# An mLSTM and mixture layer on one core: weight bytes, weights converted ahead, third tile and old-state products

## The chip, the cores and the metric

The kernel runs on one core of a Trainium2 chip. The metric is device time in microseconds of one execution, taken as a median of several runs. TensorE multiplies (PE in the rows; PEld is its weight load), VectorE (DVE), ScalarE (ACT) and GpSimd (POOL) do the rest of the arithmetic. SyncE (SP) and ScalarE issue DMAs, each from a queue of its own.

## What is computed

The reference runs an mLSTM recurrence over 768 tokens for each of 4 batches x 8 heads with a head size of 40, gates the result, and puts it through a two-layer feed-forward block.

```python
for t in range(S):
    m_new = np.maximum(f_gate[:, :, t] + m, i_gate[:, :, t])
    f_stab = np.exp(f_gate[:, :, t] + m - m_new)
    i_stab = np.exp(i_gate[:, :, t] - m_new)
    m = m_new
    C = f_stab * C + i_stab * einsum('bhd,bhe->bhde', vt, kt)
    n = f_stab * n + i_stab * kt
    h_tilde = einsum('bhde,bhe->bhd', C, qt)
    denom = np.maximum(np.abs(einsum('bhd,bhd->bh', n, qt)), 1.0)
    y[:, :, t] = sigmoid(o_gate[:, :, t]) * h_tilde / denom
h = x @ w_in                                   # (3072, 320) @ (320, 2048)
g = np.maximum(h, 0.0) + np.log1p(np.exp(-np.abs(h)))
out = (g @ w_out).astype(np.float32)           # @ (2048, 320)
```

The weights arrive as 64-bit floats and are made into f32 on the chip.

## The kernel before

*Tiles and steps.* The recurrence is cut into chunks of 128 tokens. One step is one chunk of one batch with its 8 heads, named batch_chunk: 0_1 is batch 0, chunk 1. There are 24 steps; three make a token tile of 384 tokens, and there are 8 tiles (NT), numbered from 0. `ORDER` (L38) sets which step is which: tile 0 is 1_0, 2_0, 0_0; tile 1 is 3_0, 0_1, 0_2; tile 2 is 0_3, 0_4, 0_5; the later tiles follow batches 1, 2 and 3. A step with chunk above 0 needs the state of the chunk before it.

*A step.* Decay factors are broadcast from DRAM (`fb`, L435) and scanned into a decay matrix `pw` (L444, two halves). The scores q.k (`sp`) are weighed by it (L536). The weighed scores times the gated values give `yq` (L607). Where there is an old state, its product with q (`iq`) is multiplied by the decays `y` that were loaded from DRAM (`fc_d`, L357), and `yq` is added (L613). The result `y` goes to DRAM (`yd`, L620) and comes back in the layout of the activations (`nw`, `yx`, L627 to L635). The denominator `nm` (L639 to L641) scales the gate `eg` (L644), which multiplies `yx` (L650). ScalarE casts that into X (L652), VectorE writes the remainder into X's second half (L654). The new state is `cn` (L517).

*Three forms of step.* Tile 0 (`first_tile`) has no old state and works in plain f32. Tile 1 (`mid`, `scores_pairs` and `inter_pairs`, L556 and L587) also takes q and k in f32, with two heads stacked on partitions 0 and 64. From tile 2 on (`wide`, t >= WIDE), q and k are loaded (L297), split into a high part on ScalarE (L302) and a remainder on VectorE (L308), and stacked three times by six DMAs on the chip per step (L392, L393), so that one pass of TensorE does the three products; the state is stacked and split in the same way (L326, L327, L523, L524).

*The feed-forward block.* For each tile and each of 16 slices of the hidden size, 8 matmuls make `hp` (L941), ScalarE applies softplus (L812, L816, L817), VectorE forms the remainder `gl` (L820), and `po` gathers the second layer (L912): 3 matmuls in f32 for tile 0, 9 in split form later. In tile 0's slices the weights are still on their way. There are 16 weight tensors, 8 of each layer (`wi`, `wo`), loaded by L229 into three raw buffers. Each is made into f32 words by `single` (L199): two scaled copies (L206, L212) and one operation on the top byte of each word (L210) on ScalarE, then a merge on VectorE (L215). For wi, casts and remainders follow (L239 to L249), for wo a cast (L259) and later a remainder (L268).

*What sets the order.* Every engine runs its instructions in the order in which they were written. Tile 0's beginning is ordered by the table `F`. From its first product on, `tick` counts matmuls, and attention steps, conversions, output copies and loads are generators that resume when their due count comes. The due counts are in the tables `W` (wide steps), `M` (tile 1), `Q`, `CI` and `CO` (wi and wo conversions). `tensors` (L876) is the order of the weight tensors, and the first `AHEAD` of them are converted from within `F`. The y of tile 1 has one buffer (`yy`, L352); that of a wide step shares the three raw weight buffers (L354). Tile t's products are written after all three of its steps have ended (L926).

## Time and profile before

| | |
|---|---|
| median of 3 runs | 495.15 us (490.76 to 496.38) |
| the profiled execution's own time | 490.26 us |
| its span, first to last instruction | 488.5 us |
| TensorE busy | 457.8 us (94%), 3309 matmul records |
| VectorE busy | 326.7 us (67%) |
| ScalarE busy | 226.1 us (46%) |
| GpSimd busy | 74.4 us (15%) |
| granted TensorE clock, mean | 0.962 |

Times in a row are counted from the span's start. An f32 matmul stands as two records. A wait is put down to the releaser that came last. The granted clock is a share of full speed: 1.00 is 2.4 GHz, 0.50 is 1.2 GHz.

### The profile page before, as it was taken

To read this page: it belongs to the slowest core of one execution; us is meant where nothing else is said; L and a number is where in the kernel's file an instruction comes from. 1 tells how busy PE (TensorE), PEld (TensorE's weight loads), DVE (VectorE), ACT (ScalarE), POOL (GpSimd) and SP (SyncE) were. 2 spreads that over 40 slices of the span, in tenths; PEclk is the share of its full clock that TensorE was granted. 3 is DMA by queue.
4 is the path that set the end of the run, shared out by engine and by line. 5 is a ranking of instruction groups with operands and counts; after the bars stand their busy time and mean duration, and the time that the engine had idled before them with its cause. 6 is when DMAs were issued, how large, how long until landed. Compare 5 with 4: busy or idle time off the path is not lost.

```text
span 488.5 us, 8914 instructions
## 1 busy us (share of the span) xinstructions
PE 457.8 (94%) x3309; PEld 429.0 (88%) x3309; DVE 326.7 (67%) x581; ACT 226.1 (46%) x427; POOL 74.4 (15%) x133
## 2 busy tenths in 40 slices
PE   7888988777999979999999999999998999999997
PEld 7776755566998979999999999999997999999996
DVE  5868676858699646878679667867785765642211
ACT  3469676863443523535343634264243533334232
POOL 4131301120210220310130220212031021000000
PEclk9759988988999979999999999999999999999999
DMA  6927887672686864765696666766674563001001
GB/s 223 366 82 266 265 274 232 227 216 74 189 232 177 218 176 113 215 166 169 200 250 162 202 175 186 221 192 193 167 225 125 180 185 109 16 23 42 1 1 40
DMA packets 75482, 82.79 MB, mean 169 GB/s; under 512 B 5975, under 2 KB 62191, under 8 KB 75439
## 3 DMA queue, kind: packets, MB, share of 16 engines
q1 hardware_dynamic: 55237, 72.58, 49.2%
q10 hardware_dynamic: 20202, 9.64, 8.1%
q8 instruction: 26, 0.43, 0.4%
q14 instruction: 17, 0.14, 0.1%
HBM read 54.49 MB, written 8.40 MB: 129 GB/s over the span
## 4 chain that ended last, share of the span: by engine, by line
PE 65%; DMA 17%; DVE 7%; ACT 5%; SPq 3%; issue 2%; ACTq 1%; POOL 0%; DVEq 0%
PE hp L941 28%; PE po L912 27%; DMA fb<-fz_d 3%; DMA yx<-yd 3%; PE yq L607 3%; DMA y<-fc_d 2%; PE sp L543 2%; DMA yd<-y 2%; DVE pw L444 2%; DMA kst<-hik 1%; PE yp L573 1%; DMA qst<-hiq 1%; DMA qst<-loq 1%; PE iq L547 1%; DMA nw<-yd 1%
## 5 line engine op out<-in xcount | busy, mean ns | idle before, releaser
L941 PE MATMUL hp<-X,wih 128*128 128x384 f32 x768 | 185.3, 348 | 7.4 <-ACT X L652 6.0
L941 PEld LDWEIGHTS hp<-X,wih 128*128 128x128 f32 x768 | 136.8, 192 | 11.8 <-ACT X L652 6.5
L816 ACT ACTIVATE gh<-hp 128x384 fp32r<-128x384 f32 x112 | 55.0, 491 | 192.1 <-PE hp L941 171.9
L820 DVE TENSOR_TENSOR gl<-hp,gh 128x384 fp32r<-128x384 f32 x112 | 60.8, 551 | 46.0 <-ACT hp L817 45.3
L912 PE MATMUL po<-woh,gl 128*128 128x320 f32 x336 | 70.5, 312 | 2.0 <-DVE gl L820 1.8
L912 PE MATMUL po<-wol,gh 128*128 128x320 f32 x336 | 72.2, 314 | 0.0
L912 PE MATMUL po<-woh,gh 128*128 128x320 f32 x336 | 72.0, 312 | 0.0
L941 PE MATMUL hp<-X,wil 128*128 128x384 f32 x256 | 67.7, 344 | 0.0
L912 PEld LDWEIGHTS po<-woh,gh 128*128 128x128 f32 x336 | 58.1, 189 | 0.3 <-issue 0.3
L912 PEld LDWEIGHTS po<-woh,gl 128*128 128x128 f32 x336 | 54.8, 189 | 2.8 <-DVE gl L820 2.8
L444 DVE TENSOR_TENSOR_SCAN pw<-fb,ident 128x512 f32<-128x512 f32 x48 | 56.0, 1206 | 1.2 <-PE fb L430 1.1
L912 PEld LDWEIGHTS po<-wol,gh 128*128 128x128 f32 x336 | 54.8, 189 | 0.7 <-issue 0.7
L817 ACT ACTIVATE hp<-hp 128x384 f32<-128x384 f32 x112 | 54.5, 486 | 0.0
L536 DVE TENSOR_TENSOR pw<-sp,pw 128x512 f32<-128x512 f32 x48 | 32.6, 685 | 31.4 <-PE sp L543 31.2
L327 POOL TENSOR_TENSOR cs<-cn,cs 120x336 fp32r<-120x336 f32 x15 | 14.2, 945 | 224.2 <-ACT cs L326 179.3
L941 PEld LDWEIGHTS hp<-X,wil 128*128 128x128 f32 x256 | 47.0, 191 | 0.8 <-issue 0.7
L912 PE MATMUL po<-wof,gh 128*128 128x320 f32 x96 | 33.5, 493 | 7.8 <-DVE wof L215 7.8
L912 PEld LDWEIGHTS po<-wof,gh 128*128 128x128 f32 x96 | 19.2, 211 | 16.9 <-DVE wof L215 9.1
L553 DVE TENSOR_TENSOR y<-iq,y 41x512 f32<-41x512 f32 x36 | 24.4, 679 | 1.6 <-DMA y<-fc_d 1.0
L607 PE MATMUL yq<-pw,vi 128*48 128x128 f32 (+1 forms) x336 | 23.0, 280 | 1.1 <-DVE pw L536 1.0
L457 POOL TENSOR_TENSOR vi<-vt,gT 128x328 f32<-128x328 f32 x23 | 20.3, 884 | 15.2 <-DMA vt<-in_vko 7.7
L652 ACT CAST X<-eg 128x384 fp32r<-128x384 f32 x21 | 10.7, 508 | 22.0 <-DVE eg L650 22.0
(118 smaller groups left out, 508.3 us busy)
## 6 DMA issues: line engine op xcount, KB each, us to landing
fb<-fz_d SPq DMA_DIRECT2D x44, 256.0 KB
vt<-in_vko SPq DMA_DIRECT2D x23, 324.0 KB
qst<-hiq SPq DMA_DIRECT2D x36, 160.0 KB
kst<-hik SPq DMA_DIRECT2D x36, 160.0 KB
wi<-in_wts SPq DMA_DIRECT2D x8, 640.0 KB
wo<-in_wts SPq DMA_DIRECT2D x8, 640.0 KB
eg<-in_oT SPq DMA_DIRECT2D x7, 576.0 KB
yd<-y ACTq DMA_DIRECT2D x42, 96.0 KB
```

The costliest lines, as they stand in the source:

```text
L327: nc.gpsimd.tensor_tensor(z.cs, z.old, z.cs, op=ALU.subtract)
L444: nc.vector.tensor_tensor_scan(pw.rearrange(flat), fb.rearrange(flat), ident4.rearrange(flat), 0.0, ALU.mult, ALU.add)
L457: nc.gpsimd.tensor_tensor(z.vi, v1, gT[:, z.c, z.hs].unsqueeze(2).broadcast_to([128, H, E]), op=ALU.mult)
L536: nc.vector.tensor_tensor(z.pws[i], sp, z.pws[i], op=ALU.mult)
L553: nc.vector.tensor_tensor(y, iq, y, op=ALU.mult)
L607: nc.tensor.matmul(yq[e0:e1, p, :], z.via[:, h * E : h * E + e1 - e0], z.pws[i][:, p, :], start=True, stop=True)
L652: nc.scalar.copy(X[:, 0:3, ts], z.e)
L816: nc.scalar.activation(gh, hp, AF.Softplus)
L817: nc.scalar.activation(hp, hp, AF.Softplus)
L820: nc.vector.tensor_tensor(gl, hp, gh, op=ALU.subtract)
L912: nc.tensor.matmul(po[j], a[:, j * 128 : (j + 1) * 128], w, start=first, stop=(last and left[j] == 0))
L941: nc.tensor.matmul(hp, a, r, start=(i == 0), stop=(i == len(seq) - 1))
```

## The change

Four things change, and with them the numbers of all the tables.

1. The operation on the top byte (L210) moves from ScalarE to GpSimd. It adds a large constant, so that the byte lands in the low bits of the f32 word; ScalarE then overwrites the upper half word (L212), which therefore waits for GpSimd.
2. `AHEAD` goes from 1 to 3, so two tensors of the first layer and one of the second are converted from within `F`. Tile 2's output gates are loaded and put through the sigmoid there too.
3. `PLAIN` and `WIDE` go from 2 to 3: tile 2 is treated as tile 1 is, with a table `N` of its own. Its y keeps the buffers and the DMA queue of the wide steps (`late`); tile 1's y is now written and read back through SP's queue (`queue`). Loads of q and k in this form take 104 partitions instead of 128.
4. `inter_pairs` goes. `scale_queries` multiplies q by the decays in one VectorE operation, and `values_wide` adds the old state's products to the value products in PSUM. For this the states of chunks 0_0 to 0_4 lie in two fixed tiles `chain` with zeros between the heads' blocks.

```diff
-PLAIN = 2
-WIDE = 2
+PLAIN = 3
+WIDE = 3
...
-        half = sg.bitcast(U16).rearrange("p (f w) -> p f w", w=2)
-        nc.scalar.activation(half[:, :, 0], top, AF.Copy, scale=1.0 / 32, bias=-31.0 / 64)
-        yield
-        nc.scalar.activation(half[:, :, 1].bitcast(F16), hi_w.bitcast(F32), AF.Copy, scale=2.0**-112)
+        half = sg.bitcast(F16).rearrange("p (f w) -> p f w", w=2)
+        nc.gpsimd.tensor_scalar(sg.bitcast(F32), top, -15.5, 1.5 * 2.0**28, op0=ALU.add, op1=ALU.add)
+        yield
+        nc.scalar.activation(half[:, :, 1], hi_w.bitcast(F32), AF.Copy, scale=2.0**-112)
...
-    F = dict(wm=16, g0=10, l0=19, w00=86, l1=45, g1=50, fz=71, o0=93, l2=122, lg0=15, f2=116, o1=122, w10=210,
+    F = dict(wm=16, zs=212, g0=10, l0=19, w00=46, l1=51, g1=49, fz=71, o0=93, l2=116, lg0=7, f2=116, o1=122, o2=315,
...
-            self.wide, self.mid = self.t >= WIDE, self.t == 1
+            self.wide, self.mid = self.t >= WIDE, 0 < self.t < WIDE
...
-            self.at = W if self.wide else M
-            self.split = NG <= nxt < 2 * NG
+            self.at = (M, M, N, W)[min(self.t, WIDE)]
+            self.late = self.t > 1
+            self.queue = nc.scalar if self.late else nc.sync
+            self.split = NG <= nxt < WIDE * NG
...
-            nc.sync.dma_start(z.qst, qk2[z.s, 0])
-            nc.sync.dma_start(z.kst, qk2[z.s, 1])
+            nc.sync.dma_start(z.qst[0 : PP + D], qk2[z.s, 0, 0 : PP + D])
+            nc.sync.dma_start(z.kst[0 : PP + D], qk2[z.s, 1, 0 : PP + D])
...
-    def inter_pairs(z):
-        rows = [slice(i * PP, i * PP + E) for i in range(2)]
-        iqs = [ps_a.tile([PP + E, HG, L], F32, tag="pa", name=f"iq{i}_{z.n}") for i in range(2)]
-        z.old = z.old or last_state(z)
-        for p in range(HG):
-            for i, old in enumerate(halves(z.old, True, E)):
-                q = z.qst[i * PP : i * PP + D, p, :]
-                nc.tensor.matmul(iqs[i][rows[i], p, :], old[:, p, :], q, start=True, stop=True)
-        for i in range(2):
-            yield Q["IQD"]
-            nc.vector.tensor_tensor(z.y[rows[i]], iqs[i][rows[i]], z.y[rows[i]], op=ALU.mult)
-            done.add(("iq", z.s, i))
+    def scale_queries(z):
+
+        rows = slice(0, PP + D)
+        nc.vector.tensor_tensor(z.y[rows], z.qst[rows], z.y[rows], op=ALU.mult)
+        done.add(("iq", z.s, 0))
+        done.add(("iq", z.s, 1))
...
+        joint = z.mid and z.c > 0
+        if joint:
+            need(("iq", z.s, 0))
+            z.old = z.old or last_state(z)
+        for p in range(HG):
+            rows = [(yq[i * PP : PP + i * EP, p, :], PP + i * (EP - PP)) for i in range(2)]
+            for i, (y, m) in enumerate(rows):
+                h = 2 * p + i
+                nc.tensor.matmul(y, z.via[:, h * E : h * E + m], z.pws[i][:, p, :], start=True, stop=not joint)
+            for i, (y, m) in enumerate(rows if joint else []):
+                nc.tensor.matmul(y, z.old[:, i, p, 0:m], z.y[0 : PP + D, p, :], start=False, stop=True)
...
-            nc.scalar.dma_start(rows[i], z.y[i * PP : i * PP + EP])
+            z.queue.dma_start(rows[i], z.y[i * PP : i * PP + EP])
...
-            eg[1] = p1.tile([128, NG, 3, L], F32, tag="eg", bufs=2, name="eg1")
-            nc.sync.dma_start(eg[1], oT[1])
+            for t in range(1, WIDE):
+                eg[t] = p1.tile([128, NG, 3, L], F32, tag="eg", bufs=2, name=f"eg{t}")
+                nc.sync.dma_start(eg[t], oT[t])
+                yield
+            for t in range(1, WIDE):
+                nc.scalar.activation(eg[t], eg[t], AF.Sigmoid)
+                done.add(("eg", t))
             yield
...
-    AHEAD = 1
+    AHEAD = 3
```

The change of tables and code moves instructions on every engine. Three places follow; line numbers of the changed kernel are about 6 to 16 higher than those of the same lines before.

The first is ScalarE's queue before the first product. `sgi` and `sgo` are words of a tensor of the first or second layer in the making, `eg` the output gates of a tile, `X` the activations of tile 0. Before:

```order
L693 ACTIVATE eg_172<-eg_172 128x1152
L702 ACT_TABLE_LOAD
L664 CAST X_315<-xp_0_316 128x3x128
L239 CAST wih<-sgi_258 128x2x256
L243 CAST wih<-sgi_258 64x128 x2
L664 CAST X_315<-xp_0_327 128x3x128
L664 CAST X_315<-xp_0_339 128x3x128
L206 ACTIVATE magi_356<-wi_208 128x640
L210 ACTIVATE sgi_358<-wi_208 128x640
```

And now:

```order
L718 ACT_TABLE_LOAD
L705 ACT_TABLE_LOAD
L705 ACTIVATE eg_174<-eg_174 128x1152
L705 ACTIVATE eg_299<-eg_299 128x1152
L206 ACTIVATE magi_304<-wi_210 128x640
L212 ACTIVATE sgi_310<-wi_210 128x640
L239 CAST wih<-sgi_310 128x2x256
L243 CAST wih<-sgi_310 64x128 x2
L206 ACTIVATE mago_351<-wo_176 128x640
L212 ACTIVATE sgo_353<-wo_176 128x640
L672 CAST X_339<-xp_0_340 128x3x128
L259 CAST woh<-wof_350 128x640
```

Two more weight tensors (`wi_210`, `wo_176`), a second tile of gates and a second table load stand ahead of X, and the byte operation (L210) stands nowhere.

The second is VectorE's queue in tile 0, around the merge for slices 10 and 11 (`wof_989` before, `wof_946` now). `pw_3` are the scans of step 0_3, `y_2` step 0_2's result, `X` the activations of tile 1. Before:

```order
L644 TENSOR_TENSOR eg_172<-eg_172,nm_1_945 128x384
L444 SCALAR_TENSOR_TENSOR pw_3_0_969<-fb_3_0_880,ident_79 128x512
L444 SCALAR_TENSOR_TENSOR pw_3_1_971<-fb_3_1_882,ident_79 128x512
L613 TENSOR_TENSOR y_2_825<-yq_2_959,y_2_825 112x512
L517 TENSOR_TENSOR cn_2_937<-cn_2_937,cp_2_950 40x4x41 x2
L650 TENSOR_TENSOR eg_172<-yx_1_850,eg_172 128x384
L654 TENSOR_TENSOR X_818<-eg_172,X_818 128x3x128
L215 SCALAR_TENSOR_TENSOR wof_989<-mago_990,sgo_997 128x640
```

And now:

```order
L652 TENSOR_TENSOR eg_174<-eg_174,nm_1_905 128x384
L623 COPY y_2_824<-yq_2_919 112x512
L247 TENSOR_TENSOR wil<-sgi_844,wih 128x2x256
L249 TENSOR_TENSOR wih<-sgi_844,wih 64x128 x2
L658 TENSOR_TENSOR eg_174<-yx_1_835,eg_174 128x384
L526 TENSOR_TENSOR chain_103<-chain_103,cp_2_910 40x4x41 x2
L662 TENSOR_TENSOR X_778<-eg_174,X_778 128x3x128
L215 SCALAR_TENSOR_TENSOR wof_946<-mago_947,sgo_949 128x640
```

The scans of step 0_3 have gone behind the merge (they stand six rows further down), and the remainders of a first-layer tensor have come ahead of it.

The third is SP's queue at step 0_1 of tile 1. `y_1` are its decays, `yd_0` the written result of step 3_0, `nw_0` and `yx_0` what is read back of it. Before:

```order
L229 DMA wi_580<-in_wts 128x1280
L189 DMA flast<-fl_d 104x160
L528 DMA park<-cn_0_529 40x336
L297 DMA loq_596<-in_qk 120x1024
L297 DMA lok_598<-in_qk 120x1024
L229 DMA wo_607<-in_wts 128x1280
L357 DMA y_1_612<-fc_d 64x4x128
L358 DMA y_1_612<-fc_d 48x4x128
L382 DMA qst_2_636<-in_qk 128x512
L383 DMA kst_2_637<-in_qk 128x512
L229 DMA wi_654<-in_wts 128x1280
```

And now:

```order
L229 DMA wo_622<-in_wts 128x1280
L363 DMA y_1_633<-fc_d 64x4x128
L364 DMA y_1_633<-fc_d 48x4x128
L388 DMA qst_2_637<-in_qk 104x512
L389 DMA kst_2_638<-in_qk 104x512
L189 DMA flast<-fl_d 104x160
L635 DMA nw_0_669<-yd_0_581 128x1x128
L229 DMA wi_678<-in_wts 128x1280
L641 DMA yx_0_671<-yd_0_581 128x2x128
L643 DMA yx_0_671<-yd_0_581 128x1x128
L229 DMA wo_710<-in_wts 128x1280
L628 DMA yd_1_744<-y_1_633 192x1x128 x2
```

The loads of tile 2's q and k (`loq`, `lok`) are gone, and the reads of `yd_0`, with the write of `yd_1` behind them, stand between the weight loads.

## Rows read from the trace of the kernel before

**Rows 1.** Stages: length, busy PE, PEld, DVE, ACT, POOL (x instructions), clock, DMA share, GB/s
```profile
61.90:117.20 55.30, 42.36 (x281) 31.79 (x280) 39.88 (x69) 38.73 (x61) 6.74 (x12) 0.91 0.73 226
...
173.00:182.00 9.00, 5.91 (x21) 5.90 (x21) 4.18 (x9) 1.87 (x4) 1.44 (x2) 0.62 0.74 211
182.00:228.40 46.40, 46.40 (x380) 45.32 (x380) 34.10 (x62) 20.93 (x40) 8.51 (x17) 1.00 0.62 172
...
sum 488.50, PE 457.76 PEld 428.98 DVE 326.72 ACT 226.13 POOL 74.45; mean PE 65.39 PEld 61.28 DVE 46.67 ACT 32.30 POOL 10.64
```

**Rows 2.** Timeline, TensorE: start, us, line, operation [idle before <-releaser]
```profile
64.65 1.06 PE L594 MATMUL iq<-qst,cn 40*41 40x128 f32 x14 [2.33 <-DVE pw L536]
...
100.62 4.92 PE L912 MATMUL po<-wof,gh 128*128 128x320 f32 x12 [4.52 <-DVE wof L215]
...
117.21 1.97 PE L941 MATMUL hp<-X,wih 128*128 128x384 f32 x5 [2.93 <-ACT X L652]
...
176.10 1.97 PE L941 MATMUL hp<-X,wih 128*128 128x384 f32 x5 [3.09 <-ACT X L652]
```

**Rows 3.** TensorE's busy time, granted clock, DMA share, in low stretches
```profile
66.00:69.40 3.40, 3.40 (x30) 0.50 0.96 318
...
175.20:182.00 6.80, 5.89 (x20) 0.50 0.73 217
```

**Rows 4.** Timeline, ScalarE and VectorE ahead of the wait at 100.62 us
```profile
91.15 1.16 ACT L369 ACTIVATE eg<-eg 128x1152 f32<-128x1152 f32 x1
...
92.32 1.28 ACT L371 ACT_TABLE_LOAD   x1
...
98.73 0.51 ACT L652 CAST X<-eg 128x384 fp32r<-128x384 f32 x1 [1.30 <-DVE eg L650]
...
99.75 0.82 DVE L215 SCALAR_TENSOR_TENSOR wof<-mago,sgo 128x640 uint32<-128x640 uint32 x1
```

**Rows 5.** Groups of instructions: busy us, mean ns | idle before, releasers
```profile
L607 PE MATMUL yq<-pw,vi 128*48 128x128 f32 (+1 forms) x336 | 23.0, 280 | 1.1 <-DVE pw L536 1.0
...
L543 PE MATMUL sp<-qst,kst 120*128 120x128 f32 x144 | 20.4, 264 | 0.0
...
L547 PE MATMUL iq<-qst,cs 120*41 120x128 f32 x144 | 14.6, 223 | 1.0 <-DVE y L553 1.0
...
L564 PE MATMUL sp<-qst,kst 40*128 40x128 f32 x96 | 8.8, 335 | 2.4 <-DMA kst<-in_qk 2.4
...
L210 ACT ACTIVATE sgi<-wi 128x640 uint16<-128x640 uint8 x8 | 7.4, 924 | 0.0
...
L206 ACT ACTIVATE magi<-wi 128x640 f32<-128x640 f32 x8 | 6.3, 783 | 2.3 <-DMA wi<-in_wts 2.2
...
L239 ACT CAST wih<-sgi 128x512 fp32r<-128x512 f32 x8 | 5.0, 619 | 3.6 <-DVE sgi L215 3.6
```

**Rows 6.** Timeline, GpSimd products and a VectorE merge beside one
```profile
6.94 1.94 POOL L163 TENSOR_TENSOR ig<-ig,m 32x640 f32<-32x640 f32 x1 [4.51 <-DVE m L160]
...
36.19 0.74 POOL L457 TENSOR_TENSOR vi<-vt,gT 128x328 f32<-128x328 f32 x1 [2.84 <-DMA vt<-in_vko]
...
36.31 1.30 DVE L215 SCALAR_TENSOR_TENSOR wof<-mago,sgo 128x640 uint32<-128x640 uint32 x1 [0.72 <-ACT sgo L212]
```

**Rows 7.** Timeline, VectorE and TensorE before the first product
```profile
19.21 1.28 DVE L536 TENSOR_TENSOR pw<-sp,pw 128x512 f32<-128x512 f32 x2
...
24.36 0.17 DVE L577 TENSOR_SCALAR nq<-yp 128x8 f32<-128x8 f32 x1 [1.47 <-PE yp L573]
...
31.71 0.69 PE L941 MATMUL hp<-X,wih 128*128 128x384 f32 x1 [0.57 <-ACT X L664]
```

**Rows 8.** Chain that ended last: start us, us, what
```profile
52.03 9.17 DMA yd<-y
...
195.58 1.39 PE hp L941 x8
196.97 1.32 PE po L912 x9
```

More of the change, by code (lines that the diff above doesn't have):

```diff
@@ L294, in prepare @@
         parts[t] = []
-        for nm, src in zip("qk", qk[t - 2]):
+        for nm, src in zip("qk", qk[t - WIDE]):
             lo = p1.tile([D3, H, L], F32R, tag=f"lo{nm}", name=f"lo{nm}{t}")
@@ L350, in load_decays @@
         need("fc") if z.c > 0 else None
-        if z.mid:
+        if not z.late:
             z.y = p1.tile([PP + EP, HG, L], F32, tag="yy", name=f"y{z.n}")
@@ L480, in halves @@
         if split:
-            return [tile[i * PP : i * PP + D, :, 0:e] for i in range(2)]
+            return [tile[i * PP : i * PP + D, i, :, 0:e] for i in range(2)]
         return [tile[0:D, i, :, 0:e] for i in range(2)]
     def old_state(z):
-        shape = [PP + D, HG, E2] if z.split else [D3, 2, HG, E2]
-        z.cn = p2.tile(shape, F32, tag="cn" if stays(z.b, z.c) or z.s > NG else "cs", name=f"cn{z.n}")
+        if z.split:
+            z.cn = chain[z.c % 2]
+        else:
+            tag = "cn" if stays(z.b, z.c) or z.s > NG else "cs"
+            z.cn = p2.tile([D3, 2, HG, E2], F32, tag=tag, name=f"cn{z.n}")
         z.new = halves(z.cn, z.split, E)
@@ L603, in values_wide @@
         yq = ps_a.tile([PP + EP, HG, L], F32, tag="pa", name=f"yq{z.n}")
-        for h in range(H):
-            p, i = divmod(h, 2)
-            e0, e1 = i * PP, PP + i * EP
-            nc.tensor.matmul(
-                yq[e0:e1, p, :], z.via[:, h * E : h * E + e1 - e0], z.pws[i][:, p, :], start=True, stop=True
-            )
+        joint = z.mid and z.c > 0
[9 more added lines that the diff above has]
+                nc.tensor.matmul(y, z.old[:, i, p, 0:m], z.y[0 : PP + D, p, :], start=False, stop=True)
         yield Q["YQD"]
-        if z.c > 0:
+        if z.c > 0 and not joint:
             need(("iq", z.s, 0), ("iq", z.s, 1))
@@ L626, in read_wide @@
         z.nq = p1.tile([128, L], F32, tag="sig", name=f"nw{z.n}")
-        nc.scalar.dma_start(z.nq, z.yd[DM : DM + H].partition_broadcast(128 // H))
-        if z.mid:
+        z.queue.dma_start(z.nq, z.yd[DM : DM + H].partition_broadcast(128 // H))
+        if not z.late:
             z.yx = p1.tile([128, 3, L], F32, tag="x", name=f"yx{z.n}")
@@ L669, in new_x @@
         Xs[t] = p2.tile([128, 6, T], F32R, tag="X", name=f"X{t}")
+    chain = [cpool.tile([PP + D, 2, HG, PP], F32, name=f"chain{i}") for i in range(2)]
     def first_tile():
@@ L689, in next_gates, with zeros @@
         def next_gates():
-            eg[1] = p1.tile([128, NG, 3, L], F32, tag="eg", bufs=2, name="eg1")
-            nc.sync.dma_start(eg[1], oT[1])
+            for t in range(1, WIDE):
[5 more added lines that the diff above has]
+                done.add(("eg", t))
             yield
-            nc.scalar.activation(eg[1], eg[1], AF.Sigmoid)
-            done.add(("eg", 1))
-            yield
+        def zeros():
+            for c in chain:
+                nc.gpsimd.memset(c, 0.0)
         def keep_decays():
@@ L797, in later_step @@
                 (Q["F6"] if z.s == WIDE * NG else W["FB"], fetch),
-                (Q["L9"] if z.s == (WIDE + 1) * NG else W["LOAD" if z.g else "LOAD0"], lambda: load(z)),
+                (W["LOAD" if z.g else "LOAD0"], lambda: load(z)),
                 (W["SP1"], lambda: scores(z, 1, 0)),
@@ L991, in mlstm_moe_kernel @@
         for t in range(WIDE, NT):
-            start(wide_gates([t]), TS * (t - 2) + Q["GT" if t > WIDE else "GT2"])
+            start(wide_gates([t]), TS * (t - 2) + Q["GT"])
         zs = first_tile()
```

60 lines of the change are left out of this document (32 added, 28 removed).

## The prediction

> **What bounds the kernel now.** I read the busy time by stage first, then TensorE's waits in each stage, then the other engines around those waits.
>
> TensorE is busy 457.76 of 488.5 us, but not evenly [rows 1]. From 182 to 228.4 us it is busy for all of 46.40 us at a granted clock of 1.00. Nothing off TensorE is worth anything in that stage, and it repeats for most of the span. Before it, TensorE is fed badly. From 61.9 to 117.2 us, the second part of token tile 0's products, it is busy 42.36 of 55.30 us, so idle for 12.94, at a clock of 0.91. From 173 to 182 us, around the start of tile 2, it is busy 5.91 of 9.00 us at 0.62.
>
> Its longest waits [rows 2] are of three kinds: for VectorE's merge of an output weight (wof, L215), 4.52 us at 100.62; for the weighing of an attention step (pw, L536), 2.33 us at 64.65; and for the activations X that start a tile (L652), 2.93 us at 117.21 and 3.09 us at 176.10. Behind the long waits the clock is lower. Five stretches after 61.9 us stand at 0.50: three of 3.4 us before 117 us, one of 3.4 us at 117.2, one of 6.8 us at 175.2; the first and the last of them stand in [rows 3]. Work at half clock takes twice its time, so a stretch costs half its length: 1.7 us four times, and 3.4 us.
>
> The 4.52 us wait shows why the merges are late [rows 4]. In ScalarE's queue stand a sigmoid of tile 2's output gates (1.16 us), a table load behind it (1.28 us) with a twin ahead of it, and byte operations on weights (0.92 us each, L210) [rows 5]. In VectorE's queue, ahead of the merge at 99.75 us, stand two scans for the next step and the end of step (0,1), which itself waits for ScalarE's cast of X at 98.73 us.
>
> **The change part by part.**
>
> *Byte operation to GpSimd (16 instructions of L210).* ScalarE loses 0.92 us a tensor [rows 5], 14.7 us in all, about 12 of it after the first product. GpSimd gains an operation of one strided byte input that the trace does not show. From below: a product of 328 elements with two inputs took 0.74 us [rows 6]; half the reads make 0.37, and 640 elements 0.72. From above: 640 elements with two inputs took 1.94 us [rows 6]. I take 1.0, nearer to the 0.74 row, whose shape (128 partitions) is the nearer one. GpSimd is busy 6.74 of 55.30 us in the stage [rows 1], so its idle time hides 11 to 13 of them; only ScalarE's half-word write, which now waits for GpSimd, could be held up.
>
> There is a second cost. VectorE's merge took 0.82 us at 99.75 [rows 4], but 1.30 us at 36.31, while GpSimd's product ran from 36.19 [rows 6]: 0.48 us lost to the overlap. Thirteen more GpSimd operations behind the first tensors, every second one of them meeting such a VectorE operation, make 13 x 0.5 x 0.5, about 3 us of VectorE time. I count that in what remains below. The Trainium skill ("SBUF — State Buffer", section "SBUF: two separate sides") speaks against the edit: a VectorE operation with two SBUF inputs and a GpSimd operation that reads SBUF lock each other out for a whole instruction. The overlapped merge agrees. By that rule the 13 could cost VectorE up to 13 us, which is the VectorE rival below.
>
> *Three tensors converted ahead.* Three weight tensors instead of one are converted before the first product, and two tiles' gates go through the sigmoid there, behind a softplus table load that has come ahead of them, so that a further load follows (first order piece in the section on the change). VectorE's second merge now stands ahead of the second step's denominators. The path: VectorE's first weighing pairs end at 20.49 [rows 7]; merge 0.82; casts 0.62, and two of a quarter of its elements, together as long again; two table loads 2.56; two sigmoids 2.32; conversion of the second tensor 0.78 and 0.92 [rows 4, 5]; its merge 0.82. The sum is 29.95 us. The denominators started at 24.36, so what stands behind them comes 5.5 us later, and the first product at about 37.2 instead of 31.71 us [rows 7]. From below this costs 2.5 us (had the strict chain an overlap of half of it), from above 7, if the third tensor's merge and cast, which stand among the last casts of X, come on top. I take **+5.5**. In return two tensors more are done by then.
>
> *Tile 2 in f32, old-state products in the value products.* Gone for tile 2: the split of q and k, 18 on-chip stacking DMAs, and the copies and casts of each state. VectorE has one multiplication less in each of five steps with an old state (two by iq become one by q). TensorE's work hardly moves [rows 5]: a wide step has 1.13 us of scores (20.4/18) and 0.81 of old-state products (14.6/18), an f32 step 1.47 (8.8/6) and, in the form of the value products, 1.10 (23.0/21). That is +0.63 for each of three steps. In tile 1 two steps go from 1.2 (1.06 for 14 of 16 records [rows 2]) to 1.10. Together **+1.7 us**.
>
> *SP queue.* Tile 1's y writes and reads move from ScalarE's DMA queue to SP. There the waiting DMA held conversions; here it holds weight loads and the next step's decays (third order piece). One such write took 9.17 us to land [rows 8], and SP already waited for it before it loaded the next decays, because tile 1's y buffer is single. Cost from -2 (ScalarE no longer held) to 9 us; I take 0, with the three raw weight buffers as the cover.
>
> *The sum, against the profiled execution's own 490.26 us (span 488.5).*
> - Start: +5.5.
> - Stage 61.9 to 117.2: 12.94 idle and 3 x 1.7 of low clock make 18.0 to win. The scans stand behind the merge now (second order piece), ScalarE has about 12 us less to do and no sigmoid pair, and one tensor less is left to convert. VectorE stays the fullest engine after TensorE (39.88 of 55.30 [rows 1]), so I leave a third: **-12**.
> - Start of tile 1: the 2.93 is in that stage; half of the low clock's 1.7: -0.9.
> - Start of tile 2: 3.09 and 3.4. The values of its last step now stand in product group 9 of tile 1 instead of 11, so two groups more lie between them and X, 2 x 2.71 us (1.39 + 1.32 [rows 8]), against 3.09 missing: **-6**.
> - TensorE's work: +1.7.
>
> 5.5 - 12 - 0.9 - 6 + 1.7 = -11.7, so **478.6 us**. Later tiles are bound by TensorE before and after and give nothing. The three timed runs before lie from 490.76 to 496.38 with a median of 495.15; the profiled one is 4.9 below that. I do not add the difference and leave it to the range's upper part.
>
> **The rivals.**
>
> *VectorE becomes the bound.* For: it is the next fullest engine in the stage, and each lockout with GpSimd is added there. Against: five multiplications and tile 2's split go. With 10 us lost in place of 3, 7 of the 12 won are given back: 486 us.
>
> *SP's queue takes the place of ScalarE's.* For: a write takes 9.17 us to land, and twice as many such waits now stand between weight loads. Against: loads run up to three tensors ahead. If the merges come as late as before, the 12 and the 0.9 are not won: 490.3 + 5.5 - 6 + 1.7 = 491.5 us.
>
> *GpSimd's byte operation is far dearer than any of its rows (slower).* It takes every eighth byte and converts it. Place: ScalarE's half-word write behind it, 13 times in tile 0. With 13 operations of c us and GpSimd's other 8 or so, tile 0's products end no sooner than 37 + 8 + 13c. They ended near 114, so above c = 5.5 us the stage grows, and above about 6 it takes back tile 2's 6 us too. At c = 7 tile 1 starts at 136 instead of 117, and the time is 490.3 + 19 - 6 + 1.7 = 505 us. Against: that is over three times the upper bound from rows.
>
> **How the numbers follow.** Forecast 0.64 (own range 468 to 485); VectorE 0.15 (486); SP 0.13 (491.5); GpSimd 0.08 (505). About 1% is what a measurement of this kernel can tell from no change, so faster is below 490.2 against the median of 495.15. The forecast, VectorE and 0.02 of SP's spread make 0.81 faster; 0.10 of SP the same; GpSimd with 0.01 of SP 0.09 slower. The range reaches down to 466, where all of 18.0, 1.7 and 6.5 is won, the start costs 2.5 and TensorE's work nothing (466.6), and up to 491, about SP's time.
>
> **What would show it.** Right: the first product near 37 us; no wait for wof over 2 us before tile 1; tile 1 starting between 105 and 113 us; no low clock where tile 2 starts, near 163 us; byte operations near 1 us. Wrong: tile 1 starting at 117 us or later; merges of 1.3 us and more as a rule (VectorE); weight loads that SP issues late behind y, with merges waited for as now (SP); byte operations of several us (GpSimd); a first product after 39 us.

## The result, and the profile after

The changed kernel takes 479.51 us (median of 4 runs, 478.38 to 481.38); the kernel before, run beside it, 495.76 us (490.76 to 500.64). The ratio is 0.971, with a 95% interval of 0.963 to 0.979. A control later, the changed kernel once more on another occasion, gave 479.53 us (476.09 to 480.83) and a ratio of 0.969 (0.963 to 0.975). The profiled execution took 481.38 us (span 479.6). The ratios here and below leave out disturbed executions, those over 1.5% above the fastest of their kernel, so that a ratio need not be that of the two medians.

Windows of the two traces, cut at the first product of tile 0, at the starts of tiles 1, 2 and 3, and at the end; the kernel before comes first. Columns as in [rows 1].

```profile
0.00:31.70 31.70, 25.64 (x152) 23.03 (x152) 23.04 (x49) 12.79 (x20) 10.76 (x21) 0.79 0.67 238
31.70:117.20 85.50, 70.48 (x489) 53.55 (x489) 60.28 (x104) 62.79 (x106) 13.07 (x22) 0.92 0.73 229
117.20:176.10 58.90, 54.67 (x394) 51.88 (x394) 47.82 (x81) 24.62 (x47) 8.38 (x15) 0.96 0.68 180
176.10:231.20 55.10, 55.09 (x417) 53.85 (x418) 38.09 (x71) 23.16 (x45) 9.95 (x18) 0.95 0.61 173
231.20:488.50 257.30, 251.86 (x1859) 246.66 (x1858) 157.49 (x281) 102.76 (x210) 32.30 (x57) 1.00 0.49 138
```

```profile
0.00:43.60 43.60, 25.45 (x152) 22.23 (x152) 28.05 (x56) 19.34 (x29) 21.64 (x25) 0.74 0.61 202
43.60:114.10 70.50, 66.67 (x505) 52.48 (x505) 53.91 (x90) 43.09 (x79) 44.35 (x37) 0.94 0.77 221
114.10:169.30 55.20, 54.59 (x426) 51.03 (x426) 43.68 (x77) 22.88 (x44) 6.47 (x12) 1.00 0.62 171
169.30:221.80 52.50, 52.49 (x416) 51.11 (x417) 39.20 (x73) 23.20 (x45) 10.03 (x18) 1.00 0.64 188
221.80:479.60 257.80, 252.04 (x1860) 246.69 (x1858) 155.45 (x280) 102.31 (x210) 31.32 (x57) 1.00 0.48 138
```

Read the first column down both. The start is longer by 11.9 us, the way from the first product to tile 1 shorter by 15.0, tile 1's stretch by 3.7, tile 2's by 2.6; the rest is 0.5 longer. The sum is -8.9, the difference of the spans. From the first product to tile 1, TensorE's idle time (length less PE) fell from 15.0 to 3.8 us and its busy time by 3.8. In tile 1's stretch the idle time fell by 3.6. The two profiled executions differ by 8.9 us, the two medians by 16.2: the one before was the fastest of its kernel's, the one after the slowest. So what follows accounts for the 8.9.

TensorE's waits after, the lines that answer to [rows 2]:

```profile
77.17 0.79 PE L957 MATMUL hp<-X,wih 128*128 128x384 f32 x3 [0.55 <-DVE wih L249]
...
81.85 5.19 PE L928 MATMUL po<-wof,gh 128*128 128x320 f32 x12 [1.94 <-DVE wof L215]
...
114.15 0.79 PE L957 MATMUL hp<-X,wih 128*128 128x384 f32 x3 [0.81 <-ACT X L660]
```

One wait for a merge of 1.94 us is left (2.44 in the control's profile). Tile 1 waits 0.81 us for X, and where tile 2 starts no wait is left. Against [rows 3], one stretch at a clock of 0.50 is left besides the first products, from 82.7 to 86.1 us, behind that wait.

The start after, on ScalarE, VectorE and GpSimd, to be held against [rows 7]:

```profile
28.67 2.22 ACT L705 ACTIVATE eg<-eg 128x1152 f32<-128x1152 f32 x2
...
38.89 0.92 ACT L212 ACTIVATE sgo<-wo 128x640 f16<-128x640 f32 x1 [3.70 <-POOL sgo L210]
...
18.13 4.56 DVE L450 TENSOR_TENSOR_SCAN pw<-fb,ident 128x512 f32<-128x512 f32 x4
...
22.88 1.28 DVE L545 TENSOR_TENSOR pw<-sp,pw 128x512 f32<-128x512 f32 x2
...
33.13 0.16 DVE L586 TENSOR_SCALAR nq<-yp 128x8 f32<-128x8 f32 x1
...
39.84 1.21 DVE L215 SCALAR_TENSOR_TENSOR wof<-mago,sgo 128x640 uint32<-128x640 uint32 x1 [2.15 <-ACT sgo L212]
40.97 0.73 DVE L592 TENSOR_TENSOR x<-yp,og 128x320 f32<-128x320 f32 x1
...
36.06 2.80 POOL L210 TENSOR_SCALAR sgo<-wo 128x640 f32<-128x640 uint8 x1
...
43.63 0.69 PE L957 MATMUL hp<-X,wih 128*128 128x384 f32 x1 [0.57 <-DMA wi<-in_wts]
```

The pairs of weighings that ended at 20.49 us before end at 24.16, the denominators come at 33.13, and then GpSimd's byte operation for the third tensor holds ScalarE, VectorE's merge and the third x behind it. The groups of the conversion, all 16 tensors (wait columns as in [rows 5]):

```profile
L210 POOL TENSOR_SCALAR sgo<-wo 128x640 f32<-128x640 uint8 x8 | 21.1, 2632 | 1.3 <-DVE wih L249 0.7
L210 POOL TENSOR_SCALAR sgi<-wi 128x640 f32<-128x640 uint8 x8 | 19.6, 2450 | 0.7
...
L212 ACT ACTIVATE sgo<-wo 128x640 f16<-128x640 f32 x8 | 7.4, 928 | 11.4 <-POOL sgo L210 11.4
```

The operation that cost ScalarE 0.92 us costs GpSimd 2.45 to 2.63, and ScalarE waited 11.4 us for it.

### The profile page after: what moved, and what is told of

It is laid out like the page before. It is cut to its first block, busy times and chain, and to the rows that moved or that the text cites. A ratio compares the mean times of both kernels' runs of the same rounds, so it can differ in the third digit from the quotient of the medians.

```text
span 479.6 us, 8933 instructions
## 1 busy us (share of the span) xinstructions
PE 451.2 (94%) x3357; PEld 423.5 (88%) x3357; DVE 320.3 (67%) x572; ACT 210.8 (44%) x406; POOL 113.8 (24%) x147
## 4 chain that ended last, share of the span: by engine, by line
PE 81%; DVE 7%; DMA 6%; ACT 2%; issue 2%; POOL 1%; SPq 0%; ACTq 0%; DVEq 0%; POOLq 0%
PE hp L957 36%; PE po L928 33%; PE yq L615 3%; DMA yx<-yd 3%; PE sp L552 2%; DMA y<-fc_d 2%; PE cp L517 2%; PE sp L573 2%; DVE pw L450 2%; PE iq L556 1%; PE fb L436 1%; DMA wi<-in_wts 1%; DMA kst<-in_qk 1%; DVE pw L545 1%; PE yq L617 1%
## 5 line engine op out<-in xcount | busy, mean ns | idle before, releaser
L957 PE MATMUL hp<-X,wih 128*128 128x384 f32 x768 | 182.5, 344 | 3.3 <-DVE wih L249 0.9
L957 PEld LDWEIGHTS hp<-X,wih 128*128 128x128 f32 x768 | 134.5, 189 | 7.6 <-DVE X L662 1.7
L928 PE MATMUL po<-woh,gl 128*128 128x320 f32 x336 | 72.0, 312 | 1.9 <-DVE gl L836 1.9
L928 PE MATMUL po<-woh,gh 128*128 128x320 f32 x336 | 70.0, 310 | 0.0
L331 POOL TENSOR_TENSOR cs<-cn,cs 120x336 fp32r<-120x336 f32 x12 | 11.1, 923 | 173.3 <-ACT cs L330 158.9
L928 PE MATMUL po<-wof,gh 128*128 128x320 f32 x96 | 30.2, 460 | 2.1 <-DVE wof L215 1.9
L615 PE MATMUL yq<-pw,vi 128*48 128x128 f32 (+1 forms) x336 | 24.9, 275 | 0.0
L479 POOL TENSOR_TENSOR vw<-vt,gw 128x328 f32<-128x328 f32 x19 | 17.4, 917 | 22.3 <-DVE gw L473 16.2
L210 POOL TENSOR_SCALAR sgo<-wo 128x640 f32<-128x640 uint8 x8 | 21.1, 2632 | 1.3 <-DVE wih L249 0.7
L562 DVE TENSOR_TENSOR y<-iq,y 41x512 f32<-41x512 f32 x30 | 20.3, 678 | 0.5
```

Source lines behind the costliest of these rows:

```text
L210: nc.gpsimd.tensor_scalar(sg.bitcast(F32), top, -15.5, 1.5 * 2.0**28, op0=ALU.add, op1=ALU.add)
L331: nc.gpsimd.tensor_tensor(z.cs, z.old, z.cs, op=ALU.subtract)
L479: nc.gpsimd.tensor_tensor(z.vw, v1, z.gw.broadcast_to([128, H, E]), op=ALU.mult)
L562: nc.vector.tensor_tensor(y, iq, y, op=ALU.mult)
L615: nc.tensor.matmul(y, z.via[:, h * E : h * E + m], z.pws[i][:, p, :], start=True, stop=not joint)
L928: nc.tensor.matmul(po[j], a[:, j * 128 : (j + 1) * 128], w, start=first, stop=(last and left[j] == 0))
```

## The experiments

All are the changed kernel with one edit, unless said otherwise. The tables of the order stay as they were made for the changed kernel, so what a part is worth holds for that order. Each ratio is to the kernel before, run on the same occasion; the medians come from several occasions, so differences of 2 to 3 us between them are judged by the ratios. The times:

| kernel | us, median | lowest to highest | ratio to before |
|---|---|---|---|
| changed kernel | 479.51 | 478.38 to 481.38 | 0.971 (0.963 to 0.979) |
| the same, control | 479.53 | 476.09 to 480.83 | 0.969 (0.963 to 0.975) |
| byte op on ScalarE, start only | 476.72 | 475.81 to 479.02 | 0.968 (0.961 to 0.975) |
| byte op on ScalarE, all | 476.90 | 472.66 to 478.37 | 0.966 (0.958 to 0.974) |
| kernel before, byte op on GpSimd | 501.73 | 493.13 to 506.58 | 1.008 (1.001 to 1.015) |
| second step's decays back | 477.12 | 474.75 to 478.41 | 0.965 (0.959 to 0.971) |
| one tensor ahead | 498.23 | 495.09 to 499.05 | 1.009 (1.005 to 1.013) |
| one ahead, byte op on ScalarE | 490.68 | 486.20 to 492.85 | 0.998 (0.994 to 1.003) |
| tile 1's y on ScalarE's queue | 487.48 | 485.92 to 489.87 | 0.987 (0.981 to 0.994) |
| old-state products apart | 487.10 | 484.57 to 487.93 | 0.984 (0.978 to 0.991) |
| three edits, ScalarE | 473.74 | 471.93 to 474.91 | 0.963 (0.958 to 0.968) |
| three edits, VectorE | 474.82 | 473.60 to 475.05 | 0.965 (0.960 to 0.969) |

**The byte operation by itself.** A kernel of its own. Its operations in short, each three times; then six of L156, which is as L134, beside twelve of L159:

```diff
+nc.gpsimd.tensor_scalar(a, top, -15.5, C2, op0=ALU.add, op1=ALU.add)   # L134; u8 adjacent L136, f32 L138, L140
+nc.gpsimd.tensor_copy(a, top)                                           # L142; f32 L144
+nc.gpsimd.tensor_tensor(a, f32c, f32c, op=ALU.mult)                     # L146
+nc.vector.tensor_scalar(w, top, -15.5, C2, op0=ALU.add, op1=ALU.add)    # L150
+nc.vector.scalar_tensor_tensor(g, b, 3, c, ...)                         # L152 alone, L159 beside L156
```

> This kernel leaves the whole computation out: GpSimd and VectorE run single operations on 128x640 elements, first one engine alone, then both at once. Theory: the 2.45 us of the byte operation is its own price on GpSimd, of the byte input and its stride: alone it takes 2.3 to 2.5 us, the same two additions on 640 adjacent f32 elements take 0.7 to 1.2 us. Rival: the price is that of two additions, whatever is read: the f32 form takes 2.3 us too. Second rival: it is 1.0 us by itself and the rest was VectorE's doing: alone it takes 0.7 to 1.2 us. Of the overlap: if the engines lock each other out, twelve merges of 0.82 us beside six byte operations of 2.4 us take up to 12 x 0.82 + 6 x 2.4 = 24 us together; if they only slow a little, 15 us.

Groups by form. The first two (L156, L159) ran side by side, the others alone:

```profile
L156 POOL TENSOR_SCALAR a<-r 128x640 f32<-128x640 uint8 x6 | 16.5, 2754 | 0.5
L159 DVE SCALAR_TENSOR_TENSOR g<-b,c 128x640 uint32<-128x640 uint32 x12 | 11.6, 966 | 1.0 <-POOL a L153 0.6
L134 POOL TENSOR_SCALAR a<-r 128x640 f32<-128x640 uint8 x3 | 7.1, 2375 | 1.6 <-DMA r<-in_wts 1.4
...
L140 POOL TENSOR_SCALAR a<-d 128x640 f32<-128x640 f32 x3 | 7.0, 2350 | 0.2
...
L146 POOL TENSOR_TENSOR a<-d 128x640 f32<-128x640 f32 x3 | 3.8, 1253 | 0.2
L152 DVE SCALAR_TENSOR_TENSOR g<-b,c 128x640 uint32<-128x640 uint32 x3 | 2.5, 822 | 0.1
L142 POOL CAST a<-r 128x640 f32<-128x640 uint8 x3 | 2.2, 748 | 0.2
L144 POOL COPY a<-d 128x640 f32<-128x640 f32 x3 | 2.2, 722 | 0.2
L150 DVE TENSOR_SCALAR w<-r 128x640 f32<-128x640 uint8 x3 | 1.5, 495 | 0.1
```

The first rival won: the price is that of the operation with two scalar additions, 2.35 us on adjacent f32 and 2.38 on every eighth byte. The bytes and their stride cost next to nothing: a plain cast of the same bytes took 0.75 us. Side by side, the 12 merges took 1.73 us longer in all (12 x 0.144), and the operations about 0.4 us each; the two together lasted 17 us, nearer to a small slowing than to a lockout.

**The byte operation on ScalarE in the start.**

```diff
+        if n in ("i0", "i1", "o0"):
+            nc.scalar.activation(half[:, :, 0], top, AF.Copy, scale=1.0 / 32, bias=-31.0 / 64)
+        else:
...
```

> The byte operation goes back to ScalarE for the three tensors of the start alone. Theory: GpSimd's 2.4 to 2.8 us for the third of these tensors, behind two scalings of output gates, holds ScalarE 3.7 us and with it the third x; without it the third x comes some 3 us sooner, the first product at 40 to 41 us in place of 43.6, and the time is 475 to 478 us in place of 479.5. Rival: the start is late for its other parts (the decays of the second step ahead of the first's, two table loads, two sigmoids), and what ScalarE is spared it gets back as its own 0.92 us each: the first product stays at 43 to 44 us and the time within 1 us of 479.5.

The first product came at 40.64 us and the time was 476.72, both as the theory said; and yet the theory is not borne out. The control's profile has its first product at 41.25 us, with GpSimd's operations in place. What made most of the 3 us between 43.63 and 40.64 is TensorE's speed at the very start: the first 16 score products took 2.08 us in the profile of the changed kernel, 1.16 us here and in the control, and the 24 products behind them 4.00 and 2.94. On like starts the edit saves 0.6 us. So the theory's numbers came true by luck.

**The byte operation on ScalarE throughout.** The same line for every tensor.

> The byte operation goes back to ScalarE for all 16 tensors, the rest of the change stays. Theory: ScalarE's relief carries part of the gain before tile 1; its 13 operations of 0.92 us behind the start come back, half of the 12 us lies in its idle time, tile 1 starts 3 to 6 us later measured from the first product (73 to 77 us behind it, now 70.5), and the time is 478 to 483 us. Rival: the two tensors more that are converted ahead, and the order, carry the whole gain, and GpSimd's operation is worth nothing or costs: the time is that of the kernel with ScalarE in the start alone, 475 to 478 us, or less.

476.9 us: the rival.

```profile
43.00:111.00 68.00, 65.27 (x505) 52.11 (x505) 50.96 (x89) 52.43 (x92) 12.08 (x23) 0.96 0.75 224
```

From the first product to tile 1 it took 68.0 us, less than the 70.5 with GpSimd (70.9 in the control's profile). ScalarE was busy for 52.4 of those 68.0 us and could carry the operations. Tile 1's stretch is 1.5 us longer (56.7 against 55.2), which takes back part of it. The times of this run and of the one before it overlap the control's, and so do the ratios (0.966 and 0.968 against 0.969): that the kernel is faster without GpSimd's operation is not shown, and no run shows a gain from having it.

**The kernel before with GpSimd's operation alone.**

> The kernel before with the byte operation on GpSimd for all 16 tensors and nothing else changed. Theory: ScalarE's relief counts by itself, the waits for merged output weights before tile 1 become shorter (4.52 us at 100.62 to under 3 us), and the time falls by 2 to 6 us. Rival: 2.45 us on GpSimd in place of 0.92 us on ScalarE makes each conversion 1.5 us longer, with one tensor ahead the products wait for it: the time rises by 2 to 8 us.

By the ratio the time rose by 0.8% (0.1 to 1.5), some 4 us, by the medians of all executions by 1.4%: the rival in its direction, with an uncertain size. The runs with one tensor ahead, below, show the waits behind it.

**The second step's decays back in their place.** `f1=158` becomes `f1=174` in the table `F`.

> The decays of the second attention step of tile 0 go back behind those of the first (one number of the order table); nothing else changes. Theory: their place ahead of the first step's is why VectorE's four scans began at 18.13 us in place of 14.46 (TensorE's fb had to wait for a scan to free a PSUM buffer), all that follows in the start hangs on it, so the first pairs of weighings end at about 20.5, the first product starts at 39.5 to 41 us in place of 43.63, and the time is 475 to 478 us. Rival: the first product hangs on ScalarE's and GpSimd's work on the three tensors, not on the scans; it stays within 1 us of 43.6 and the time within 1 us of 479.5.

The first product stayed at 43.13 us: the rival for the start. The time lies in the theory's range all the same, but not for the theory's reason: in this profile the stretch from tile 1 to the end, which the edit does not touch, is 3.2 us shorter than the changed kernel's (362.3 against 365.5). The chain found another late link at once, the third step's decays from DRAM:

```profile
14.24 2.33 DVE L450 TENSOR_TENSOR_SCAN pw<-fb,ident 128x512 f32<-128x512 f32 x2
18.84 1.23 DVE L450 TENSOR_TENSOR_SCAN pw<-fb,ident 128x512 f32<-128x512 f32 x1 [2.27 <-DMA fb<-fz_d]
20.95 1.23 DVE L450 TENSOR_TENSOR_SCAN pw<-fb,ident 128x512 f32<-128x512 f32 x1 [0.88 <-DMA fb<-fz_d]
```

The first scans are back at 14.24 us (14.46 before), but the last one starts at 20.95, and the pairs end at 23.65 in place of 24.16.

**One tensor ahead.** `AHEAD = 3` becomes 1, and `K0` -8 becomes -16.

> One tensor is converted ahead of the first product in place of three; the second starts eight products earlier in the order than the changed kernel's first late one, since its input weights are needed there. Theory: the two tensors more carry the gain before tile 1. Without them the first product comes at 33 to 36 us, but the merges are late by two conversions again, GpSimd's 2.4 us in each: TensorE waits 8 to 15 us for merged weights before tile 1, tile 1 starts at 118 to 126 us, and the time is 484 to 492 us. Rival: the gain comes from the new order and from ScalarE's relief; the stage keeps its 70.5 us behind the first product, tile 1 starts at 104 to 108 us, and the time is 469 to 474 us.

498.23 us, above the theory's range and far from the rival's. The first product came at 35.15 us, tile 1 at 131.7. TensorE waited 11.9 us for merged output weights on the way. The longest of these waits, and the start of tile 1:

```profile
94.88 4.91 PE L928 MATMUL po<-wof,gh 128*128 128x320 f32 x12 [7.16 <-DVE wof L215]
...
131.70 1.45 PE L957 MATMUL hp<-X,wih 128*128 128x384 f32 x5 [1.19 <-ACT X L660]
```

**One tensor ahead, byte operation on ScalarE.**

> One tensor converted ahead (as in the run with 498.2 us) and the byte operation on ScalarE for all tensors. Theory: what the two tensors more ahead are worth is large by itself, and GpSimd's 2.4 us adds to it only where conversions are what TensorE waits for: from the first product to tile 1 it takes 84 to 92 us (96.5 with GpSimd's operation and one ahead, 68.0 with ScalarE's and three ahead), and the time is 487 to 494 us. Rival: the tensors ahead are worth something only as a cover for GpSimd's slow operation; with ScalarE's operation one ahead is enough: 70 to 76 us to tile 1, and 468 to 476 us. Second rival: GpSimd's operation plays no part, and the time stays at 496 to 500 us.

490.68 us: the theory, and 88.3 us from the first product to tile 1 as well:

```profile
34.40:122.70 88.30, 70.86 (x506) 54.84 (x506) 52.68 (x94) 58.23 (x102) 12.12 (x23) 0.90 0.63 194
```

Together with two runs above this is a table of two by two, by medians: GpSimd's operation costs 7.5 us with one tensor ahead and 2.6 with three (the 2.6 is not clear of noise); the two tensors more bring 18.7 us with GpSimd's operation and 13.8 with ScalarE's. With one tensor ahead and ScalarE's operation, all else of the change (the f32 form of tile 2, the joined products, SP's queue, the order) comes out at the time of the kernel before, but by another way. Tile 1 starts 5.5 us later (122.7 against 117.2), and from there to the end it takes 365.0 us against 371.3, as long as the changed kernel (365.5). So what the change wins behind the start of tile 1 does not need the tensors ahead; ahead of tile 1 this order, made for three tensors, loses it again. No run has an order made for one, so the 18.7 and 13.8 may be too high for the tensors alone.

**Tile 1's y on ScalarE's queue.** `self.queue = nc.scalar` for every step.

> Tile 1's y writes and reads go back from SP's queue to ScalarE's. Theory: on SP they cost nothing; on ScalarE they hold conversions behind a wait for VectorE's y, so the time is 479.5 to 484 us. Rival: on SP they hold weight loads and decays; back on ScalarE the time falls by 2 us or more, below 477.5.

487.48 us, 8 us above the control and more than the theory allowed. ScalarE's timeline, and TensorE's:

```profile
95.92 1.26 ACTq L628 DMA_DIRECT2D yd<-y  x2
97.23 0.81 ACT L206 ACTIVATE mago<-wo 128x640 f32<-128x640 f32 x1 [4.84 <-DMA fb<-fz_d]
...
119.64 0.51 ACT L660 CAST X<-eg 128x384 fp32r<-128x384 f32 x1 [5.05 <-DVE eg L658]
...
120.21 2.24 PE L957 MATMUL hp<-X,wih 128*128 128x384 f32 x5 [3.48 <-ACT X L660]
```

Behind the write of y (L628), which waits for VectorE's y, a conversion waits 4.84 us; its line names a DMA as the releaser, but the write stands right ahead of it in ScalarE's queue. Merges come late (TensorE waits 2.47 us at 102.03), and tile 1 waits 3.48 us for X, with a clock of 0.50 behind it.

**Old-state products apart.** In `scale_queries` and `values_wide`:

```diff
-        nc.vector.tensor_tensor(z.y[rows], z.qst[rows], z.y[rows], op=ALU.mult)
...
+        for i in range(2):
...
+            for p in range(HG):
+                nc.tensor.matmul(iq[rows[i], p, :], z.old[r, i, p, 0:E], z.qst[r, p, :], start=True, stop=True)
+            nc.vector.tensor_tensor(z.y[rows[i]], iq[rows[i]], z.y[rows[i]], op=ALU.mult)
...
-        joint = z.mid and z.c > 0
+        joint = False
```

> In tiles 1 and 2 the old-state products go back into PSUM tiles of their own, with two VectorE multiplications by the decays and an addition for each of the five steps with an old state, in place of one multiplication and products added into the value products; the f32 form of tile 2 stays. Theory: the joining matters little for TensorE (2 us more or less) and saves VectorE some 5 us in the stretches around tile 1, where it has cover: the time is 479 to 483 us. Rival: the joining carries the gain where tile 1 and tile 2 start; without it a wait of 2 us or more for X stands ahead of tile 2 again, with a granted clock of 0.5 behind it, and the time is 485 us or more.

487.10 us, the rival's time, but not in its place: tile 2's start has no wait. The wait and the low clock stand at tile 1:

```profile
44.80:119.70 74.90, 67.30 (x506) 52.35 (x506) 56.52 (x92) 43.00 (x80) 44.19 (x37) 0.97 0.74 214
119.70:123.20 3.50, 2.93 (x10) 2.62 (x11) 1.97 (x5) 0.14 (x1) 0.00 (x0) 0.68 0.98 229
119.70:178.30 58.60, 58.03 (x426) 53.57 (x426) 45.26 (x79) 22.68 (x44) 6.42 (x11) 0.97 0.56 153
```

```profile
119.69 0.79 PE L962 MATMUL hp<-X,wih 128*128 128x384 f32 x3 [2.35 <-ACT X L665]
```

The way to tile 1 is 4.4 us longer (74.9 against 70.5), VectorE 2.6 us busier on it; tile 1's stretch is 3.4 us longer, all of it TensorE's busy time (58.03 against 54.59), part of it the low clock.

**Three edits together.** Byte operation on ScalarE throughout, `f1=174`, and `o1s=319`, which puts the softplus load behind the two sigmoids.

> The changed kernel with the byte operation on ScalarE for all tensors, the decays of the second step behind those of the first, and the softplus table's load behind the two sigmoids of the start. Theory: each takes a piece off the chain that the start hangs on: the byte operations 1 us, one table load 1.28 us, the decays 0.5 us; the first product comes at 40 to 41.5 us, tile 1 68 to 70 us behind it, and the time is 473 to 476 us. Rival: the pieces lie beside each other, with the third step's decays from DRAM late and the third tensor's merge as the end of the start; the first product stays at 42.5 us or more and the time within 1 us of 476.9.

473.74 us: the theory's range, and below every run of the changed kernel. By the medians it is 1.2% faster than that; by the ratios to the kernel before (0.963 against 0.969 and 0.971) the difference is 0.6 to 0.8%, and the intervals overlap. Only one table load (1.28 us) stands in ScalarE's start, though the second sigmoid now waits 1.43 us for its input. The first product came at 40.94 us, 0.3 sooner than in the control with a like start, and tile 1 68.8 us later (70.9 in the control). So what gain there is comes with ScalarE's operation on the way to tile 1 more than with the start, and the theory's account of the start is not shown.

**The same with VectorE for the three of the start.**

> As the run before it, but the three byte operations of the start run on VectorE, where one took 0.50 us by itself in place of 0.92 on ScalarE and 2.37 on GpSimd; the other 13 stay on ScalarE. Theory: ScalarE's chain in the start loses two of them, 1.8 us, against 0.5 us each on a VectorE that waited 3.8 to 4.6 us there; the first product comes 1 to 2 us sooner than with ScalarE's, and the time is 471 to 475 us. Rival: VectorE ends the start with the third tensor's merge, the third x and the casts, and pays what ScalarE saves: within 1 us of the run before it.

474.82 us, 1.1 us above the run before it, whose times it overlaps. That lies in the theory's range and just outside the rival's 1 us; the rows decide for the rival. The second step's denominators came 0.9 us sooner than in that run (31.63 against 32.51 us), but the third tensor's merge 1.0 us later (38.53 against 37.52), with ScalarE waiting for VectorE's byte operation:

```profile
37.58 0.92 ACT L215 ACTIVATE sgo<-wo 128x640 f16<-128x640 f32 x1 [3.89 <-DVE sgo L211]
```

The first product came at 41.53 us, in a profile with the slower start (below).

**The control.**

> The changed kernel itself once more, as a control for the runs that differ from it by 2 to 3 us. Theory: it comes out where it did, 478 to 481 us, so that 476.7 and 476.9 us (byte operation on ScalarE in the start, and everywhere) and 477.1 us (decays in their old order) are gains of about half a per cent, and 473.7 us one of more than 1%. The scan pairs at the start begin near 18.1 us where TensorE's first products run at a clock of 0.5, near 15.8 us where they do not. Rival: its time moves by 2 us or more between chips, 475 to 477.5 us; then those three runs show no difference from it, and the last a smaller one.

It came out where it did: 479.53 against 479.51 us. The theory also expected a clock of 0.5 in the first products of the slower start. A window there reads 1.00 in both profiles (6.7 to 10 us), but the clock records of the two traces begin only later, at 11.0 us in the changed kernel's and at 5.5 us in the control's, and a window ahead of the first record reads 1.00 for want of one. The rows tell more. First the changed kernel's first score products, then the control's:

```profile
6.74 2.08 PE L573 MATMUL sp<-qst,kst 40*128 40x128 f32 x16 [0.70 <-DMA kst<-in_qk]
```

```profile
6.60 1.16 PE L573 MATMUL sp<-qst,kst 40*128 40x128 f32 x16 [0.73 <-DMA kst<-in_qk]
```

And the same 16 products later in the kernel before, at a recorded clock of 1.00 and of 0.50, with the window of the second:

```profile
13.60 1.16 PE L564 MATMUL sp<-qst,kst 40*128 40x128 f32 x16
...
18.34 2.08 PE L564 MATMUL sp<-qst,kst 40*128 40x128 f32 x16 [1.67 <-DMA kst<-in_qk]
```

```profile
18.34:20.42 2.08, 2.08 (x16) 1.78 (x16) 2.08 (x8) 0.00 (x0) 0.74 (x1) 0.50 1.02 422
```

So the slower start is one at half clock, as the theory had it. In all the kernels' profiles the first score products take 2.08 us where the clock records begin at 10.6 us or later, and 1.16 where they begin at 6.1 or earlier. The profiles before and after that are compared above both have the slower start.

## Why the prediction was right, and where it was not

The forecast of 478.6 us was right within 1 us of the measured median, and within 3 of the profiled execution (481.38). That is closer than its terms were, and partly luck. One term was 6.4 us too small, and the others together 3.6 us too careful. And the sum began at an execution 4.9 us below the median before: it forecast 11.7 us off, while the profiled executions differ by 8.9 and the medians by 16.2.

*Start, +5.5.* Measured +11.9 us between the two profiles, beyond the bound of 7. Two steps failed. The first is the anchor of the sum, "VectorE's first weighing pairs end at 20.49": it took what lies ahead of the three tensors as unmoved. The order of two steps' decays had been turned round as well, the pairs ended at 24.16, 3.7 us later, and with the order turned back the third step's decays from DRAM were late instead. From there to the denominators the sum held: 20.49 to 29.95 was worked out as 9.46 us, and 24.16 to 33.13 is 8.97. The second is that the third tensor was put at nothing, with a bound of 1.5 us. It cost 3.2: from the denominators to the first product took 7.35 us before and 10.5 now, ScalarE waiting 3.70 of them for GpSimd. On ScalarE that tensor would cost much the same, 0.6 us less.

*GpSimd's operation, 1.0 us, bounds 0.72 to 1.94.* It took 2.45 to 2.63, outside the bounds. The step that failed is "half the reads make 0.37": it priced an operation by what it reads. An operation with two scalars is dearer here than one with two tensors, 2.35 us against 1.25 on the same 640 elements. The single overlap was sized rightly: 0.48 us was taken for it, and the kernel of single operations gives 0.43 (1.73 us over about four operations). The Trainium skill ("SBUF — State Buffer", section "SBUF: two separate sides") has an exclusive lock for the whole instruction. The runs do not agree: a merge beside an operation of 2.75 us lost 0.43 us and did not wait for its end. The row on which the prediction said "The overlapped merge agrees" could not tell the two apart: GpSimd's product had only 0.6 us left when that merge began.

*VectorE as the bound* did not come. On the way to tile 1 it was busy 53.91 us against 60.28 before, and the merges that met GpSimd's operation lost about 1 us in all (6 x 0.18, against 0.82 alone), not 10:

```profile
L215 DVE SCALAR_TENSOR_TENSOR sgi<-magi,sgi 128x640 uint32<-128x640 uint32 x6 | 6.0, 999 | 2.3 <-ACT sgi L212 2.3
L215 DVE SCALAR_TENSOR_TENSOR wof<-mago,sgo 128x640 uint32<-128x640 uint32 x6 | 4.9, 822 | 3.6 <-ACT sgo L212 3.6
```

*The slower rival* named the right mechanism and a price that lay too high; at 2.5 us it stands below its own point of decision (5.5 us). With one tensor ahead it did decide: alone it made the kernel before 0.8% slower, and it is the difference between 490.7 and 498.2 us.

*Stage, -12 of 18.* The forecast's stretch began at 61.9 us; the comparable ones are those from the first product to tile 1, which begin earlier: 85.5 against 70.5 us, so -15.0, in which the wait for X at tile 1 is counted as in the forecast. The third that was left to VectorE was too much. Of the reasons given, "ScalarE has about 12 us less to do" did not carry it: with these 12 us back on ScalarE the way is 2.5 us shorter still. What carried it is the two tensors more: without them, in this order, the way is 96.5 us long, and 88.3 with ScalarE's operation. The price of 0 for SP's queue was wrong as well, in sign: SP does not cost, ScalarE's release is worth 8 us of the whole, four times the bound of -2. The reason stood in the text ("There the waiting DMA held conversions"); its size was not worked out. The joined products are worth another 7.6 us, where the forecast counted only VectorE's saved multiplications as cover and 1.7 us for TensorE.

*Tile 1 and tile 2.* The low clock at tile 1 (-0.9 taken) is gone altogether. The wait for X and the low clock at tile 2, -6 in the sum, are gone as forecast: tile 1's stretch is 3.7 us shorter and tile 2's 2.6, together 6.3, against -0.9 - 6 + 1.7 = -5.2. The reason given, two product groups more ahead of X, is not shown: no run takes the f32 form of tile 2 away. TensorE's work stands where it was put: tile 1's stretch has the same busy time as before (54.59 against 54.67) though it lost 1.7 us of low clock.

*What would show it.* No low clock at tile 2: right. No wait for wof over 2 us: right in the profile of the changed kernel (1.94) and not in the control's (2.44). Tile 1 at 114.15 us in place of 105 to 113, tile 2 at 169.3 in place of 163, a first product after 39 us, and byte operations of 2.5 us: four signs said that terms were wrong, and a forecast judged by its total alone would have hidden them.

The worth of the parts does not add up. Taken away one at a time, the two tensors cost 18.7 us, SP's queue 8.0, the joining 7.6; together 34, where the whole change brings 16. So the worths overlap: each is measured with the others in place and with tables made for all of them. That the stage then waits for whichever chain is last would explain it, and is not shown by a run of its own.

## What to carry to other kernels

When an operation moves to another engine, take its price from a row of that engine with the same kind of operands, scalars included; reads alone do not give it. Where tables of an order are rewritten, a sum over a start must begin at the first instruction that moved, not at the first one that the change is about. A queue whose DMA waits is priced by what stands behind it on its engine, on the old queue as on the new one. And two profiles of a start can be compared only where the same first products took the same time.

## What the runs showed that was not expected

On GpSimd, 128x640 elements with two scalar additions took 2.35 us, a product of two tensors 1.25, a copy or a cast from bytes 0.72 to 0.75; VectorE did the first in 0.50. The Trainium skill ("GPSIMD Engine Reference", section "4.1 Engine selection") calls operations with one input there roughly line-rate; the cast agrees, the operation with two scalars does not.

TensorE's first products ran at one of two speeds in executions of one kernel, 2.08 and 1.16 us for 16 score products, which are their times at a granted clock of 0.50 and of 1.00. Half the clock cost these products 1.8 times the time, where the prediction took twice. Single profiles of a start therefore differ by some 2.4 us (43.63 and 41.25 us to the first product) without any edit. In both, TensorE's 12 products before had run from 2.67 to 5.44 us; why the clock rose later in the one stays open.

From tile 1 to the end, too, profiles differ without an edit there: 365.5 us in the changed kernel's, 364.9 in the control's, 362.3 in that with the second step's decays back. A gain of 2 to 3 us in one profile is therefore first to be looked for in the stretch that was edited.
